# Loading the values of the first 14 attention heads over GpSimd's DMA queue instead of SyncE's

## The chip, the cores and the metric

The kernel runs on one core of a Trainium2 chip. Five engines work side by side: TensorE (PE, with its weight loads listed apart as PEld), VectorE (DVE), ScalarE (ACT), GpSimd (POOL) and SyncE (SP). SP does no arithmetic here; it issues transfers. The metric is device time in microseconds (us), the median of several runs.

## The reference, cut to what matters

Attention over 4 batches, 8 heads, 576 tokens and 64 numbers a head, with a causal mask and a decay bias, and behind it two feed-forward layers of 512 to 2048 to 512 over all 2304 tokens.

```python
scores = scale * q @ k.T
cum = cumsum(maximum(s, 0))
scores = where(causal, -1e9, scores + minimum(-(cum_i - cum_j), 0))
attn = softmax(scores)
x = (attn @ v) laid out as [B*S, H*D]
h = x @ w1_in;  x = (h * clip(h + 3, 0, 6) / 6) @ w1_out
h = x @ w2_in;  out = (h * sigmoid(h)) @ w2_out
```

## The kernel before, in words

Attention goes in head-parts: part A of a head is its first 256 query rows against the first 256 keys, part B the rest. The parts run in the order A0 A1 A2 B0 A3 B1 B2 B3 (the digit is the batch), eight heads each. A list of `Head` objects holds them, and a slot of the main loop carries one head through its stages while its neighbours are in other stages: the scores of the current head (`score`, L518), mask, scale and row maximum (`soft`, L540), exponentials (`expo`, L558), transposes of the head before (`trans`, L586), its product with the values (`av_whole`, L693), and the sum into the layer's input (L700, L711). In the same slot the heads two places ahead are loaded.

The first 9 slots carry heads only. From then on each slot also holds one step of the first feed-forward layer (`first`, L266 to L268, and `second`, L305 to L307), which takes most of TensorE's time. Weights arrive as 64-bit words, 512 KB a chunk (128 rows of 512), in `Chunk.load` (L147), and are turned into pairs of 32-bit parts by ScalarE (`fields`, L159, L160), GpSimd (L162) and VectorE (`join`, L178, L182, and `low`, L193). These ticks of the `Feed` are spread over the slots: three before the loop, 0.4 in each of the first nine slots, then two in each.

For the first 14 heads (`self.at < 14`) queries, keys and values go into one tile named `in...`, which lies in a place that weights will fill later; nothing has used it before, so the loads into it wait for no reader. A head's loads are the queries (L419), the keys (L420), the values (L409: 128 rows of 2 x 64 numbers, 64 KB) and, in `load_cum`, two rows that carry the decay (L429: from `pairs` in the on-chip memory for the first four heads, from `pair_d` in DRAM for the rest). The score matmul reads queries, keys and those two rows; only `av_whole`, a slot later, reads the values.

All loads so far go out on SP's queue, one after the other. The program is written through a layer that puts in the waits and that plans the order of each engine's instructions before the run, from the written order and from its own forecast of when each is ready. So what is ready early can stand early: the fills of `one` and `neg` in `split_rows` (L366, L367) are written behind the tenth slot. At run time every engine takes its instructions strictly in the planned order.

At the start 34 matmuls on a constant tile (`keep_clock`, L86) keep TensorE busy, and later slots without a feed-forward step add three each.

Of the kernel before, what the change touches and what calls it, by code (L numbers as in the profile page):

```python
# [27 lines left out]
def kernel(  # L28
# [15 lines left out]
    nc = tc.nc  # L44
# [85 lines left out]
    class Chunk:  # L130
# [10 lines left out]
        def load(self):  # L141
            if self.src.dtype == F32:
                self.val = self.place([P, DM], F32, "raw")
                nc.sync.dma_start(self.val, self.src)
            else:
                raw = self.place([P, 2 * DM], I32, "raw")
                nc.sync.dma_start(raw, self.src.bitcast(I32))  # L147
                words = raw.rearrange("p (n two) -> p n two", two=2)
                self.words = words[:, :, 0], words[:, :, 1]
# [226 lines left out]
    class Head:  # L376
# [23 lines left out]
        def load(self):  # L400
            b, h, nm, nk, nq = self.b, self.h, self.nm, self.nk, self.nq
            if self.at < 14:

                t = wpool.tile([P, 2 * DM], F32, tag=spare[self.at], name=f"in{nm}")
                self.q2, self.k2 = t[:, :nq], t[:, nq : nq + nk]
                self.qk = t[:, : nq + nk]
                self.va = t[:, DM + nk :][:, : self.nkc * D].rearrange("p (c d) -> p c d", d=D)
                self.load_qk()
                nc.sync.dma_start(self.va, v1[b, h, :, : self.nkc, :])  # L409
                return  # L410
            tags = ("qs", "kl") if self.whole and self.slot else ("q2", "k2")
            self.q2 = apool.tile([P, nq], F32, tag=tags[0], name=f"q2{nm}")
            self.k2 = apool.tile([P, nk], F32, tag=tags[1], name=f"k2{nm}")
            self.load_qk()
# [877 lines left out]
```

## Time and profile before

| what | us |
|---|---|
| median of 3 runs | 997.79 |
| lowest and highest run | 996.33, 1000.38 |
| time of the profiled execution | 999.31 |
| its span, first to last instruction | 997.5 |

| engine | busy us | share of the span |
|---|---|---|
| PE | 971.2 | 97% |
| PEld | 892.8 | 89% |
| DVE | 736.0 | 74% |
| ACT | 511.1 | 51% |
| POOL | 270.6 | 27% |

The first table holds the time to beat and what the profiled execution adds around its span (1.8 us). The second is an average over the whole run, over stages with different limits, so it does not tell what the first 45 us wait for; the changed loads all fall into those. SP has no busy time of its own; its issues stand in a timeline.

### The profile page before, as it was taken

The page shows a single profiled execution, that of the slowest core. Times are in us where ns is not written, and L with a number is a line of the kernel's source. Part 1 is how long each engine was busy: PE and PEld are TensorE (multiplying, and loading weights), DVE is VectorE, ACT ScalarE, POOL GpSimd, SP SyncE. Part 2 cuts the span into 40 slices and gives each one's busy share as a digit, 9 for nine tenths or more (in the row PEclk, how much of TensorE's full clock was granted, in tenths as well). Part 3 has the DMA queues.
Part 4 walks back from the last instruction along what each step waited for, and adds up shares of the span by engine and source line. Part 5 has one row for each costly group of instructions (what it writes and reads, how often), then busy time and mean ns, then how long its engine had stood idle before and what let it go on. Part 6 is the DMA issues. An engine that isn't in the chain of part 4 may idle for free.

```text
span 997.5 us, 17936 instructions
## 1 busy us (share of the span) xinstructions
PE 971.2 (97%) x6268; PEld 892.8 (89%) x6268; DVE 736.0 (74%) x1757; ACT 511.1 (51%) x1177; POOL 270.6 (27%) x323
## 2 busy tenths in 40 slices
PE   8899999999999999999999999999999999999997
PEld 5788899999999999999997877898988989889996
DVE  6899998898789888988867799887564434743343
ACT  5899655555455555545446656564443323432332
POOL 2123434343333434434325566532000000000000
PEclk8999999999999999999999999999999999999999
DMA  5785112212222222222215957434354233442421
GB/s 178 244 275 187 41 56 86 79 51 61 87 71 77 68 60 92 60 71 74 59 50 187 393 201 245 156 116 190 138 190 169 79 143 113 165 154 77 148 75 64
DMA packets 54419, 125.41 MB, mean 126 GB/s; under 512 B 12332, under 2 KB 34076, under 8 KB 51000
## 3 DMA queue, kind: packets, MB, share of 16 engines
q1 hardware_dynamic: 53880, 123.60, 36.8%
q8 instruction: 50, 0.82, 0.3%
q10 hardware_dynamic: 448, 0.66, 0.2%
q14 instruction: 41, 0.34, 0.1%
HBM read 99.52 MB, written 24.69 MB: 125 GB/s over the span
## 4 chain that ended last, share of the span: by engine, by line
PE 69%; DVE 11%; issue 7%; POOL 5%; DMA 4%; SPq 2%; ACT 1%; POOLq 0%; DVEq 0%; ACTq 0%
PE a L1089 6%; PE a L1090 6%; PE a L1091 6%; PE h L1072 5%; PE h L1074 5%; PE h L1073 5%; PE ph L266 4%; PE ph L267 4%; PE ph L268 4%; PE acc L306 4%; PE acc L305 4%; PE acc L307 4%; PE poB L678 3%; POOL rawo L167 2%; DMA rawi<-in_w2i_dram 2%
## 5 line engine op out<-in xcount | busy, mean ns | idle before, releaser
L266 PE MATMUL ph<-xh,wi 128*128 128x256 f32 (+1 forms) x512 | 152.7, 300 | 3.8 <-DVE g L279 3.6
L306 PE MATMUL acc<-gl,wo 128*128 128x256 f32 (+1 forms) x512 | 151.5, 298 | 1.4 <-DVE gl L286 1.4
L267 PE MATMUL ph<-xl,wi 128*128 128x256 f32 (+1 forms) x512 | 150.8, 295 | 0.3 <-DVE xl L732 0.3
L268 PE MATMUL ph<-xh,wi 128*128 128x256 f32 (+1 forms) x512 | 150.5, 294 | 0.0
L307 PE MATMUL acc<-gh,wo 128*128 128x256 f32 (+1 forms) x512 | 150.2, 295 | 0.0
L1131 ACT ACTIVATE gh<-h 128x384 fp32r<-128x384 f32 x96 | 50.3, 524 | 185.1 <-DVE h L1139 185.0
L305 PE MATMUL acc<-gh,wo 128*128 128x256 f32 (+1 forms) x512 | 143.4, 296 | 0.0
L1089 PE MATMUL a<-wo,gh 128*128 128x512 f32 x288 | 113.5, 394 | 1.4 <-ACT gh L1131 0.9
L1090 PE MATMUL a<-wo,gh 128*128 128x512 f32 x288 | 113.1, 393 | 0.0
L266 PEld LDWEIGHTS ph<-xh,wi 128*128 128x128 f32 x512 | 96.3, 188 | 9.1 <-DVE g L279 2.6
L306 PEld LDWEIGHTS acc<-gl,wo 128*128 128x128 f32 x512 | 96.5, 188 | 5.7 <-DVE gl L286 2.5
L267 PEld LDWEIGHTS ph<-xl,wi 128*128 128x128 f32 x512 | 96.4, 188 | 3.5 <-DVE xl L732 0.5
L307 PEld LDWEIGHTS acc<-gh,wo 128*128 128x128 f32 x512 | 96.5, 189 | 3.4
L268 PEld LDWEIGHTS ph<-xh,wi 128*128 128x128 f32 x512 | 96.5, 188 | 3.1
L305 PEld LDWEIGHTS acc<-gh,wo 128*128 128x128 f32 x512 | 95.3, 188 | 3.6 <-DVE gh L122 0.2
L1091 PE MATMUL a<-wo,gl 128*128 128x512 f32 x288 | 90.0, 392 | 0.0
L1133 DVE TENSOR_TENSOR gl<-h,gh 128x384 fp32r<-128x384 f32 x96 | 53.8, 560 | 39.9 <-ACT h L1132 38.2
L1139 DVE TENSOR_TENSOR h<-h,u 128x384 f32<-128x384 f32 x72 | 40.1, 556 | 53.5 <-PE h L1074 53.2
L114 POOL TENSOR_SCALAR gh<-g 128x512 fp32r<-128x512 f32 x68 | 50.5, 745 | 100.6 <-DVE g L279 87.5
L1072 PE MATMUL h<-x0t,w 128*128 128x384 f32 x192 | 64.9, 338 | 0.7 <-DVE u L1139 0.7
L1073 PE MATMUL h<-x1t,w 128*128 128x384 f32 x192 | 64.9, 338 | 0.0
L1074 PE MATMUL h<-x0t,w 128*128 128x384 f32 x192 | 64.7, 337 | 0.0
(222 smaller groups left out, 2522.6 us busy)
## 6 DMA issues: line engine op xcount, KB each, us to landing
w<-w_d SPq DMA_DIRECT2D x18, 1792.0 KB
w_d<-w SPq DMA_DIRECT2D x8, 1792.0 KB
k2B<-in_kT_dram SPq DMA_DIRECT2D x64, 144.0 KB
rawi<-in_w1i_dram SPq DMA_DIRECT2D x16, 512.0 KB
rawo<-in_w1o_dram SPq DMA_DIRECT2D x16, 512.0 KB
rawi<-in_w2i_dram SPq DMA_DIRECT2D x16, 512.0 KB
rawo<-in_w2o_dram SPq DMA_DIRECT2D x16, 512.0 KB
q2B<-in_qT_dram SPq DMA_DIRECT2D x64, 80.0 KB
```

The source lines that it names most:

```text
L266: nc.tensor.matmul(o, wih[:, cs], xh[c], start=c == 0, stop=False)
L267: nc.tensor.matmul(o, wih[:, cs], xl[c], start=False, stop=False)
L268: nc.tensor.matmul(o, wil[:, cs], xh[c], start=False, stop=c == NDC - 1)
L305: nc.tensor.matmul(a, woh[:, cs], gh[:, jj, :], start=b0, stop=False)
L306: nc.tensor.matmul(a, woh[:, cs], gl[:, jj, :], start=False, stop=False)
L307: nc.tensor.matmul(a, wol[:, cs], gh[:, jj, :], start=False, stop=b1)
L1072: nc.tensor.matmul(ps, w[:, 0, cs], xh[:, c, :], start=c == 0, stop=False)
L1073: nc.tensor.matmul(ps, w[:, 0, cs], xl[:, c, :], start=False, stop=False)
L1074: nc.tensor.matmul(ps, w[:, 1, cs], xh[:, c, :], start=False, stop=c == 1)
L1089: nc.tensor.matmul(accs[t], gh[:, k, cs], woh, start=b0, stop=False)
L1090: nc.tensor.matmul(accs[t], gh[:, k, cs], wol, start=False, stop=False)
L1091: nc.tensor.matmul(accs[t], gl[:, k, cs], woh, start=False, stop=b1)
```

## The change: which engine issues the load of the values

For the 14 heads, the load of the values is issued by GpSimd instead of SyncE. Source, destination and size stay the same, and so do all other loads.

```diff
                 self.load_qk()
-                nc.sync.dma_start(self.va, v1[b, h, :, : self.nkc, :])
+                nc.gpsimd.dma_start(self.va, v1[b, h, :, : self.nkc, :])
                 return
```

## Rows read from the trace of the kernel before

**Rows 1.** Busy time of each engine by stage: us busy (instructions), granted clock, DMA share, GB/s.
```profile
10.00:20.00 10.00, 7.86 (x47) 5.36 (x46) 9.04 (x34) 8.78 (x26) 1.90 (x3) 0.98 0.57 172
20.00:30.00 10.00, 9.62 (x52) 8.63 (x53) 6.37 (x26) 6.82 (x21) 1.25 (x2) 0.68 0.53 146
30.00:45.00 15.00, 12.32 (x92) 10.77 (x91) 12.38 (x50) 13.34 (x40) 2.49 (x4) 1.00 0.83 265
60.00:80.00 20.00, 18.48 (x144) 17.45 (x145) 19.84 (x61) 19.04 (x48) 4.29 (x6) 1.00 0.88 292
80.00:120.00 40.00, 37.16 (x305) 35.44 (x304) 38.70 (x93) 29.66 (x70) 14.95 (x19) 1.00 0.32 105
120.00:200.00 80.00, 78.94 (x652) 77.55 (x650) 71.68 (x198) 44.12 (x113) 30.84 (x46) 1.00 0.24 70
```

**Rows 2.** SP's issues in order of time: start, duration, line, tile loaded.
```profile
2.44 0.58 SPq L409 DMA_DIRECT2D inA<-in_v_dram  x1
4.22 0.58 SPq L409 DMA_DIRECT2D inA<-in_v_dram  x1
4.85 0.43 SPq L147 DMA_DIRECT2D rawi<-in_w1i_dram  x1
...
6.41 1.39 SPq L429 DMA_DIRECT2D inA<-pairs  x2
...
11.26 0.48 SPq L419 DMA_DIRECT2D inA<-in_qT_dram  x1
...
15.54 0.43 SPq L147 DMA_DIRECT2D rawo<-in_w1o_dram  x1
16.01 0.29 SPq L429 DMA_DIRECT2D inA<-pair_d  x1
...
19.62 0.58 SPq L409 DMA_DIRECT2D inA<-in_v_dram  x1
```

**Rows 3.** The changed line: durations minimum, median, maximum in ns, first and last start.
```profile
L409 SPq DMA_DIRECT2D inA<-in_v_dram x14: 578/584/1502, 2.4 to 43.3; - x14
```

**Rows 4.** The chain that ended last, two pieces of its first 60 us: start, duration.
```profile
5.80 5.44 DMA rawi<-in_w1i_dram
...
15.54 4.06 DMA rawo<-in_w1o_dram
```

**Rows 5.** All engines in order of time; in brackets the idle time before and its releaser.
```profile
2.89 0.50 POOL L96 TENSOR_SCALAR_AFFINE_SELECT cmask<-cmask 128x128 f32<-128x128 f32 x1
...
4.66 0.74 DVE L355 COPY pairs<-orow 32x256 f32<-32x256 f32 x1
4.68 0.57 POOL L367 MEMSET neg<- 32x576 f32 x1 [0.77 <-DVE orow L351]
...
9.77 0.67 POOL L162 TENSOR_SCALAR rawi<-rawi 128x512 f32<-128x512 f32 x1 [4.53 <-DMA rawo<-in_w1o_dram]
...
10.48 0.69 DVE L178 SCALAR_TENSOR_TENSOR magi<-magi,rawi 128x512 int32<-128x512 int32 x1 [4.07 <-POOL rawi L162]
...
11.24 0.30 PEld L518 LDWEIGHTS ps0A<-inA 66*128 66x128 f32 x2 [0.56 <-DMA rawi<-in_w1i_dram]
...
19.76 0.77 PE L518 MATMUL ps0A<-inA 66*128 66x128 f32 x2 [0.93 <-DVE wi L193]
```

**Rows 6.** Busy time of each engine in shorter stretches, columns as in the first group.
```profile
2.00:4.00 2.00, 2.00 (x7) 0.62 (x5) 1.30 (x2) 0.01 (x1) 1.91 (x5) 1.00 0.38 107
8.00:10.00 2.00, 2.00 (x11) 0.94 (x10) 0.00 (x0) 1.46 (x3) 0.23 (x1) 1.00 1.03 395
...
18.00:20.00 2.00, 0.74 (x4) 0.46 (x4) 1.55 (x9) 1.28 (x4) 0.00 (x0) 0.91 0.74 237
18.00:28.00 10.00, 8.74 (x43) 7.61 (x42) 6.46 (x30) 6.26 (x18) 0.65 (x1) 0.66 0.55 166
20.00:26.00 6.00, 6.00 (x25) 5.33 (x26) 3.44 (x14) 3.30 (x12) 0.65 (x1) 0.50 0.56 166
```

**Rows 7.** The second step of VectorE's join before 40 us: durations minimum, median, maximum in ns.
```profile
L182 DVE CUSTOM_DVE_ANT_0 magi<-rawi,magi x3: 680/684/1074, 11.2 to 31.7; 128x1024 uint16<-128x1024 uint16 x3
```

## The prediction, made before the change was run

> **What bounds the kernel now.** First I read the busy time by stage. From 120 us on TensorE has hardly any idle time (78.94 of 80 us), and from 60 to 120 us VectorE has hardly any (19.84 of 20, 38.70 of 40) [rows 1]. These two stages are long and the changed loads do not lie in them. The loads lie between 2.4 and 43.3 us [rows 3], and there no engine is full: VectorE works 9.04, 6.37 and 12.38 us in the stretches of 10, 10 and 15 us, so it stands idle for 7.2 us of the 35 [rows 1]. As VectorE is the limit right behind this stage and TensorE right behind that, a microsecond won or lost before 45 us should reach the end nearly whole, and nothing won elsewhere would.
>
> So the question is what the first 45 us wait for. The timeline of SP's queue is the second view: issue stands behind issue, about 0.04 us apart, and a load of values costs 0.584 us of it in the median [rows 3]. The chain of waits says the same: between the starts of two weight chunks it runs through SP's own issues, not through arithmetic, and it holds two transfers, one from 5.80 to 11.24 and one from 15.54 to 19.60 [rows 4]. Twice an SP issue starts as such a transfer ends, at 11.26 and at 19.62 [rows 2, 4]; each is the eighth issue behind that weight chunk, so I read it as a limit of eight transfers under way on this queue.
>
> The third view is the timeline of all engines around these two moments. The first scores start at 11.24, as the last of three weight chunks lands [rows 4, 5]; the decay rows they need were issued at 6.41, behind those chunks [rows 2]. The scores of the fifth head start at 19.76 after 0.93 us of an idle TensorE [rows 5]. The profile names a VectorE instruction as releaser, but the decay rows of this head were issued at 16.01, right behind the chunk that lands at 19.60 [rows 2, 4], and I hold that transfer for the cause. In that stretch TensorE had worked only 0.74 of 2 us, and from 20 to 26 us its granted clock is 0.50, the level of 1.2 GHz instead of 2.4, with TensorE busy 6.00 of 6 us and VectorE only 3.44 [rows 6].
>
> **The change, part by part.** Removed: 14 issues of 0.584 us and a gap of 0.04 us, 8.7 us of SP's queue in all [rows 3]. What of it lies on the path goes by where they stand.
>
> *The start.* Two loads of values stand ahead of the first weight chunk at 4.85 [rows 2]. Without them the chunks go out 2 x 0.62 = 1.2 us earlier, and the decay rows at 5.4 instead of 6.41, as VectorE's copy into their source ends at 4.66 + 0.74 = 5.40 [rows 2, 5]. At 2 to 4 us the transfers run at 107 GB/s with the DMA engines busy 0.38 of the time, at 8 to 10 us at 395 GB/s with a share of 1.03 [rows 6]: the start of the scores is set by when these chunks enter and by what shares the engines with them. That takes something back. A values load waits for nothing, and the planned order puts ready work early on POOL: its fill for a far later slot runs at 4.68 [rows 5]. So I expect POOL to issue several of the 14 loads before 10 us. At 64 KB each and 395 GB/s one costs 0.17 us of the full DMA engines; six more than now cost 1.0 us. The first scores come between 1.2 and 0.2 us earlier. I take 0.6.
>
> *The fifth head.* Five values loads stand ahead of the chunk at 15.54, so it and the decay rows behind it go out up to 5 x 0.62 = 3.1 us earlier. The decay rows then land at about 16.6 and TensorE need not stand idle at 18.8. That is 0.9 us. If TensorE then also stays at the upper clock, its 6.00 us of work at half clock shrink by up to 3.0. Both together are bounded by VectorE, whose idle time from 18 to 28 us is 10 - 6.46 = 3.5 us [rows 6]. So the term lies between 0.9 and 3.5; I take 2.4, nearer to the upper end, because TensorE's work in the stretch is full while VectorE's is not.
>
> *Behind 28 us.* VectorE stands idle for another 2.6 us from 30 to 45 [rows 1], but SP's queue has caught up there and the DMA share is 0.83, so faster issue finds fewer free engines. I take 0, and 2.6 for the far end of the range.
>
> Added: 14 issues on POOL. No row shows one. Below stands the same transfer on SP, 0.584 us in the median, above SP's slowest one, 1.50 us [rows 3]. I take 1.0, between them, thus 14 us on an engine that works 1.90, 1.25 and 2.49 us of the 35 from 10 to 45 [rows 1]. So the room is there, and I cost the added issues at nothing; what hides them is POOL's idle time, and the price where they stand ahead of POOL's part of the weights is the first slower rival below. The page DMA: Bandwidth & Descriptors of the Trainium skill, section Specifications, gives a first byte after about 1 us from GpSimd and 0.6 us from SP; by that, as an estimate, POOL's sum would be 14 us too, and no run here shows it yet.
>
> The values themselves are needed last: the product reads them a slot behind the scores, so even some microseconds of delay on POOL's queue lie behind the head's other stages.
>
> The sum is 0.6 + 2.4 = 3.0 us, made against this execution's 999.31 us (its span of 997.5 and 1.8 around it), so 996.3. The median of the runs is 997.79, 1.5 lower; on that scale the forecast is 994.8.
>
> **The rivals.**
>
> *Hidden anyway (997.2).* The clock falls nevertheless, because TensorE has too little to do before 20 us whatever the loads do, or the planned order changes and gives the time back; only the 0.6 at the start stays. For it speaks that VectorE is already busy 9.04 of 10 us just before [rows 1], so scores ready earlier wait for it too. Against it speaks the idle TensorE at 19.76.
>
> *All idle time filled (991.1).* 0.6 + 3.5 + 2.6 = 6.7 us. For it speaks that VectorE's list of work is fixed and that SP paced everything before 31 us; against it the DMA share of 0.83 to 0.88 behind 30 us.
>
> *POOL comes late (slower, about 1002).* VectorE's join at 10.48 waits for POOL's instruction at 9.77 [rows 5], and VectorE's order is fixed, so all masks and scores behind it stand too. POOL's fills with a bearing on this end at 2.89 + 0.50 = 3.39, so there are 6.4 us of room. With n values loads planned ahead of that instruction and t us for one, it decides from n x t = 6.4: with 7 ahead from t = 0.91, with all 14 from 0.46. With 7 at 1.50 the delay is 4.1 us (1001.9); with 14 at 1.0 it is 7.6 (1005.4). Against it: the order is planned with POOL's part of the weights as the older work, which goes first once it is ready.
>
> *VectorE is held by POOL (slower, 1003).* VectorE's copy at 4.66 takes 0.74 us and ends just after POOL's fill beside it (4.68 + 0.57 = 5.25) [rows 5], and a step of the join takes 1074 ns once beside 684 in the median [rows 7]. If each of the 14 loads costs VectorE the 0.39 us between these two, that is 5.5 us. The Trainium skill, page SBUF — State Buffer, section Who interferes with whom, has a rule that goes the same way: descriptor generation on GpSimd and those VectorE modes that use both ports exclude each other, so that whichever starts second waits. By it the load could also be the one that waits. The copy at 4.66 agrees with the rule; for a load no run here shows it yet. Against the rival: most of VectorE's long instructions here have two inputs or read TensorE's results, and the copy is the one full-width copy of its kind.
>
> **How the numbers follow.** Chances: forecast 0.45, hidden 0.26, all filled 0.12, POOL late 0.13, VectorE held 0.04. The bound for a difference that a measurement of this kernel can tell is 0.5%, 5 us (the three runs differ by 0.4%): 992.8 and 1002.8. The forecast's own bounds run from 1.1 us (0.2 + 0.9) to 4.7 us (1.2 + 3.5), 996.7 to 993.1; a fifth of it may fall under 992.8 with the noise of a median. With all filled that makes 0.21 faster. Of the slower rivals some end just under 1002.8: 0.13 slower, and 0.66 the same. The range reaches from 990.0 (a little beyond all filled) to 1001.5 (POOL late by a little less than 4.1 us).
>
> **What would show it.** Right: 14 issues on POOL, most before 25 us, of about 1 us each; the first weight chunk issued at 3.6 and the first scores at about 10.6; the fifth head's scores without an idle TensorE ahead of them; a granted clock near 1.00 from 20 to 26 us; VectorE idle under 2 us from 18 to 28, and the stage from 60 to 120 us the same length, only earlier. Wrong: a join of VectorE that waits for POOL for longer than now, a values load that TensorE's product waits for, a clock that falls elsewhere, or a later stage in another order with gaps of its own.

## The result and the profile after

The changed kernel takes 1008.53 us (median of 4 runs, 1004.49 to 1011.66) against 997.30 for the kernel before in the same comparison: a ratio of 1.0103, 95% interval 1.0074 to 1.0132. The forecast was 994.8 with a range up to 1001.5, so the change is slower by 1% where no measurable difference was forecast, and the time lies outside the range. The profiled execution of after took 1006.26 us, 6.95 more than that of before.

The changed line first: instances, durations in ns, first and last start, and the time from issue to landing. Its counterpart of before is [rows 3].

```profile
L409 POOL DMA_DIRECT2D inA<-in_v_dram x14: 534/534/745, 3.3 to 13.8; - x14
...
DMA to landing us min/median/max: 2.0/4.7/5.8
```

POOL in order of time (start, duration, idle time before it). [rows 5] has its weight instruction L162 at 9.77.

```profile
3.35 4.45 POOL L409 DMA_DIRECT2D inA<-in_v_dram  x8
8.18 0.53 POOL L409 DMA_DIRECT2D inA<-in_v_dram  x1 [0.38 <-issue]
10.13 0.53 POOL L409 DMA_DIRECT2D inA<-in_v_dram  x1 [1.43 <-issue]
11.21 1.08 POOL L409 DMA_DIRECT2D inA<-in_v_dram  x2 [0.54 <-issue]
...
13.32 1.06 POOL L409 DMA_DIRECT2D inA<-in_v_dram  x2
14.40 0.68 POOL L162 TENSOR_SCALAR rawi<-rawi 128x512 f32<-128x512 f32 x1
15.03 0.67 POOL L162 TENSOR_SCALAR rawo<-rawo 128x512 f32<-128x512 f32 x1
15.65 0.65 POOL L162 TENSOR_SCALAR rawi<-rawi 128x512 f32<-128x512 f32 x1
```

All 14 loads stand ahead of POOL's first weight instruction. Eight go out back to back; POOL stands idle before the ninth, tenth and eleventh, 2.3 us in all.

SP's issues, in the places of [rows 2]: the first weight chunk at 3.72 (4.85 before), the fourth at 14.12 (15.54).

```profile
3.72 0.59 SPq L147 DMA_DIRECT2D rawi<-in_w1i_dram  x1
...
5.44 1.40 SPq L429 DMA_DIRECT2D inA<-pairs  x2
...
14.12 0.59 SPq L147 DMA_DIRECT2D rawo<-in_w1o_dram  x1
```

SP is relieved as intended. Yet the first scores start at 11.22, where they started at 11.24 [rows 5]; and the chain of waits holds a transfer of 6.94 us from 4.82 where [rows 4] has 5.44 us from 5.80:

```profile
11.22 0.30 PEld L518 LDWEIGHTS ps0A<-inA 66*128 66x128 f32 x2 [1.22 <-DMA inA<-pairs]
```

```profile
4.82 6.94 DMA rawi<-in_w1i_dram
```

VectorE in order of time shows the largest difference:

```profile
11.86 0.29 DVE L540 CUSTOM_DVE_ANT_0 pb0A<-ps0A,cmask 128x128 f32<-128x128 f32 x1 [5.45 <-PE ps0A L518]
...
14.57 0.29 DVE L540 CUSTOM_DVE_ANT_0 pb0A<-ps0A,cmask 128x128 f32<-128x128 f32 x1 [1.30 <-PE ps0A L518]
...
17.68 0.42 DVE L540 CUSTOM_DVE_ANT_0 pb1A<-ps1A,cmask 128x256 f32<-128x256 f32 x1 [1.15 <-PE ps1A L518]
...
24.15 0.69 DVE L178 SCALAR_TENSOR_TENSOR magi<-magi,rawi 128x512 int32<-128x512 int32 x1
24.75 0.69 DVE L178 SCALAR_TENSOR_TENSOR mago<-mago,rawo 128x512 int32<-128x512 int32 x1
```

The first join of weights stood at 10.48 [rows 5] and now stands at 24.15, behind the scores of the first seven heads. It does not wait for POOL there: POOL was done with that chunk at 15.08, and no idle time stands before the join. Its place in VectorE's planned order has changed. In the meantime VectorE waits for scores, three times for more than a microsecond.

Busy time by stage, columns as in [rows 1] (PE, PEld, DVE, ACT, POOL, granted clock, DMA share, GB/s):

```profile
10.00:20.00 10.00, 7.99 (x44) 6.16 (x42) 4.25 (x24) 7.25 (x23) 5.58 (x10) 0.83 0.75 216
20.00:30.00 10.00, 9.18 (x64) 7.31 (x62) 9.19 (x37) 7.68 (x24) 0.00 (x0) 0.92 0.68 210
30.00:45.00 15.00, 12.31 (x63) 10.46 (x63) 14.53 (x45) 13.41 (x35) 4.60 (x6) 0.73 0.92 278
45.00:60.00 15.00, 12.10 (x56) 11.16 (x55) 15.00 (x41) 14.81 (x37) 3.25 (x4) 0.53 1.01 370
60.00:80.00 20.00, 16.82 (x133) 15.46 (x132) 19.97 (x53) 19.41 (x44) 5.64 (x8) 1.00 0.73 249
80.00:120.00 40.00, 36.19 (x295) 34.61 (x295) 39.88 (x105) 28.53 (x73) 12.54 (x15) 1.00 0.13 36
120.00:200.00 80.00, 79.88 (x667) 78.96 (x666) 67.54 (x181) 39.04 (x100) 30.99 (x42) 1.00 0.25 70
```

VectorE works 4.25 of the ten us from 10 to 20, where it worked 9.04. From there to 80 us it is nearly full (14.53 of 15 from 30 to 45, before 12.38). The granted clock from 30 to 45 and from 45 to 60 is 0.73 and 0.53; before it was 1.00 from 30 to 45 [rows 1] and beyond, as rows below show.

The whole stretch from 10 to 60 us, before and then after:

```profile
10.00:60.00 50.00, 43.13 (x287) 36.69 (x285) 42.76 (x149) 42.76 (x116) 9.29 (x13) 0.93 0.73 223
```

```profile
10.00:60.00 50.00, 41.59 (x222) 35.09 (x220) 42.97 (x144) 43.16 (x116) 13.44 (x20) 0.73 0.87 280
```

VectorE does as much work by 60 us as before, 42.97 us of it where it did 42.76. What differs is what that work is: the weight steps L178, L182 and L193 take 9.69, 8.02 and 8.54 us where they took 8.19, 8.25 and 7.54, and the heads get less. TensorE loses 1.5 us of busy time and runs at a mean granted clock of 0.73 instead of 0.93.

How the two are linked is to be seen at 34 to 38 us. VectorE:

```profile
33.98 1.16 DVE L178 SCALAR_TENSOR_TENSOR magi<-magi,rawi 128x512 int32<-128x512 int32 x1
35.07 0.68 DVE L182 CUSTOM_DVE_ANT_0 mago<-rawo,mago 128x1024 uint16<-128x1024 uint16 x1
35.67 0.28 DVE L700 TENSOR_TENSOR xtA<-poA,sums 128x128 f32<-128x128 f32 x1
35.87 0.68 DVE L178 SCALAR_TENSOR_TENSOR mago<-mago,rawo 128x512 int32<-128x512 int32 x1
...
36.54 0.68 DVE L182 CUSTOM_DVE_ANT_0 magi<-rawi,magi 128x1024 uint16<-128x1024 uint16 x1
37.14 0.41 DVE L122 COPY xA<-pxA 128x256 f32<-128x256 f32 x1
```

TensorE beside it:

```profile
36.00 0.44 PE L711 MATMUL pxA<-ident,xtA 128*128 128x128 f32 x2 [1.08 <-DVE xtA L700]
37.61 0.33 PE L586 MATMUL pt0A<-ident,pb0A 128*128 128x128 f32 x1 [0.84 <-DVE xA L122]
```

The head's small VectorE steps (L700, L122) stand behind late weight work (L178, L182), and TensorE waits for them. From 30 to 62 us it waits 5.4 us for these two where it waited 2.4 (for VectorE in all 5.4 and 3.9). It does not wait for the fuller transfers (DMA share 1.01 from 45 to 60): from 30 to 125 us TensorE waits for no transfer at all, before for 0.3 us. Shorter stretches, after and then before:

```profile
34.00:38.00 4.00, 2.08 (x14) 1.51 (x13) 4.00 (x9) 3.22 (x10) 0.60 (x1) 1.00 0.80 222
38.00:58.00 20.00, 16.39 (x68) 14.39 (x67) 19.69 (x56) 19.41 (x48) 4.86 (x6) 0.52 1.02 363
```

```profile
38.00:58.00 20.00, 16.32 (x122) 14.55 (x121) 18.93 (x55) 18.51 (x47) 4.95 (x6) 1.00 0.87 277
```

After TensorE had worked 2.08 of 4 us, the granted clock fell to 0.52 in the mean of the next 20 us, that is to 1.2 GHz for nearly all of them. TensorE is busy for the same time there, 16.39 and 16.32 us, and 68 matmuls stand in its record instead of 122. 16.39 x (1 - 0.52) = 7.9 us of full-speed work are missing after this stretch.

Following the same instructions through both traces: the scores of heads five to eight come 1 to 4 us earlier than before. The products with the values (L693) are on par at 31 us, and the one that ran at 41.8 runs at 48.9, 7.1 us late. The first feed-forward step is late by 9.2 (rows of its gate, the ScalarE instruction that reads its product, before and then after):

```profile
L278 ACT ACTIVATE g<-ph,half x13: 452/466/688, 44.0 to 119.5; 128x256 f32<-128x256 f32 x8, 128x512 f32<-128x512 f32 x5
```

```profile
L278 ACT ACTIVATE g<-ph,half x11: 452/472/691, 53.3 to 117.0; 128x256 f32<-128x256 f32 x8, 128x512 f32<-128x512 f32 x3
```

Up to 215 us the steps stay late by 8 to 13.5 us while the heads catch up; from 260 us on, where TensorE is full, the lag is 7.1 us, and the two spans differ by 6.9. TensorE's idle time and low clock, summed up in the next section, exceed those of before only up to 120 us, so this execution's loss is made there. The other 4 us between the medians lie in executions without a profile.

### The profile page after: what moved, and what is told of

The parts are those of the page before. It is cut to its first block, busy times and chain, and to the rows that moved or that the text cites. A ratio compares the mean times of both kernels' runs of the same rounds, so it can differ in the third digit from the quotient of the medians.

```text
span 1004.5 us, 18006 instructions
## 1 busy us (share of the span) xinstructions
PE 975.5 (97%) x6268; PEld 898.3 (89%) x6268; DVE 737.4 (73%) x1757; ACT 510.6 (51%) x1177; POOL 279.3 (28%) x337
## 4 chain that ended last, share of the span: by engine, by line
PE 73%; DVE 11%; DMA 6%; issue 4%; POOL 3%; SPq 2%; ACT 1%; DVEq 0%; POOLq 0%; ACTq 0%
PE a L1089 6%; PE a L1090 6%; PE a L1091 6%; PE h L1072 5%; PE h L1074 5%; PE h L1073 5%; PE ph L266 5%; PE ph L267 5%; PE acc L306 5%; PE ph L268 4%; PE acc L307 4%; PE acc L305 4%; PE poB L678 4%; POOL rawo L167 2%; DMA rawi<-in_w2i_dram 2%
## 5 line engine op out<-in xcount | busy, mean ns | idle before, releaser
L266 PEld LDWEIGHTS ph<-xh,wi 128*128 128x128 f32 x512 | 97.4, 190 | 7.0 <-DVE g L279 2.3
L268 PEld LDWEIGHTS ph<-xh,wi 128*128 128x128 f32 x512 | 97.6, 191 | 3.1
```

The costliest lines, as they stand in the source:

```text
L266: nc.tensor.matmul(o, wih[:, cs], xh[c], start=c == 0, stop=False)
L268: nc.tensor.matmul(o, wil[:, cs], xh[c], start=False, stop=c == NDC - 1)
```

## Experiments

Ratios are to the kernel before, with 95% intervals. For each profile I also sum what TensorE loses from 10 to 280 us: in stretches of 2 us, its idle time and its busy time x (1 - granted clock). Before this is 16.1 us (12.8 idle and 3.3 at the low clock, 1.2 GHz), after it is 27.2 (15.5 and 11.7). The sum is a rough measure: its difference is 11.1 us where these two executions differ by 6.95, and that the medians differ by 11.2 does not confirm it. By this measure most of the loss, 8.4 of 11.1, is made at the low clock.

**Only the order on POOL undone.** The loads stay on GpSimd but stand behind its weight instruction written last (`last_pool` holds it; the line that sets it is left out here).

```diff
+with tc.issue_after(last_pool[0].ins) if last_pool else ExitStack():
     nc.gpsimd.dma_start(self.va, v1[b, h, :, : self.nkc, :])
```

> All 14 values loads on GpSimd as in the change, but each load written after a GpSimd weight instruction (L162) is planned behind it, so VectorE's joins of the first weight chunks stand again ahead of or between the first heads' scores. Theory order (the planned order costs the time): VectorE busy over 8 us between 10 and 20 us, 994 to 999 us, no slower than before. Theory queue (a load issued by GpSimd itself costs the time, by its descriptors or its lateness): 14 such loads as in the change, so 1004 to 1010 us. Theory SP (SyncE running ahead costs the time): also 1004 to 1010 us.

Measured: 1005.42 us, 1.0073 [1.0052, 1.0095]. The first join is back at 9.6 us, so it was the loads standing ahead of POOL's weight work that had moved it:

```profile
9.61 0.69 DVE L179 SCALAR_TENSOR_TENSOR magi<-magi,rawi 128x512 int32<-128x512 int32 x1 [3.20 <-DMA inA<-pairs]
```

(The join is L179 in this run.) But the time did not come back: the theory of the order missed, and the time lies in the range of the two theories that blame the loads on GpSimd or SP's relief. VectorE is at work for 6.52 us from 10 to 20, not for the 8 that were expected. It has 11 halves of weights (L193, the last step of a chunk's preparation) ahead of the first step where before had 6 and the changed kernel 9, and TensorE is at the low clock for 20.5 us between 30 and 60.

**Only the loads on POOL added.** SP loads the values as before; GpSimd loads as many bytes into a place that nobody reads.

```diff
 nc.sync.dma_start(self.va, v1[b, h, :, : self.nkc, :])
+spare_v = t[:, DM : DM + self.nkc * D].rearrange("p (c d) -> p c d", d=D)
+nc.gpsimd.dma_start(spare_v, v1[b, h, :, : self.nkc, :])
```

> Values loaded by SyncE as before; in addition GpSimd issues 14 loads of the same size into an unused part of the same tiles. VectorE's first join is planned behind the scores of five heads. Theory order: slower than before though SyncE does all it did, 1001 to 1008 us, VectorE idle over 3 us between 10 and 20 us. Theory queue: slower too, 1003 to 1010 us. Theory SP: as before, 995 to 1000 us.

Measured: 1006.26 us, 1.0074 [1.0048, 1.0100]. The theory of SP's relief (995 to 1000) missed. The first join starts at 26.8 us, the first step is 9.4 us late (changed kernel 9.2), and the stages resemble those of the changed kernel:

```profile
10.00:20.00 10.00, 6.93 (x30) 5.26 (x29) 3.04 (x17) 6.69 (x20) 5.00 (x9) 0.75 0.71 203
...
30.00:45.00 15.00, 11.38 (x77) 8.77 (x76) 15.00 (x55) 13.63 (x41) 3.39 (x4) 1.00 0.77 222
45.00:60.00 15.00, 12.97 (x57) 11.27 (x55) 14.60 (x43) 14.98 (x38) 4.94 (x6) 0.54 1.01 326
```

So the loads on POOL are enough for most of the loss, without SP's relief. With one caution: this run moves 0.9 MB more than the others.

**Only SP relieved.** The 14 loads are left out; the product with the values reads the mask instead, so these heads' output is not attention.

```diff
-nc.sync.dma_start(self.va, v1[b, h, :, : self.nkc, :])
+self.va = cmask[:, : self.nkc * D].rearrange("p (c d) -> p c d", d=D)
```

> No load of values for the 14 heads at all; the product reads the mask tile in their place, so SyncE has 14 issues less and GpSimd none more. VectorE's joins are planned ahead of the scores as before. Theory order: 993 to 998 us, about the 3 us faster that were forecast. Theory queue: the same. Theory SP: slower, 1004 to 1010 us, as SyncE runs ahead just as in the change.

Measured: 1001.63 us, 1.0046 [1.0025, 1.0067]. Without any of the 8.7 us of issue that the change takes from SP the kernel is not faster; the time lies between the expected ranges, and all three theories missed. Here too 11 halves of weights stand ahead of the first step, which starts 4.9 us late; its lag from 260 us on is only 0.6, so the profile shows little of the 4 us, and where the rest is lost stays open.

**Only VectorE's order changed.** The loads are as before; VectorE's joins of the first four chunks are held behind the softmax reduction (L540) written last (`last_soft`; the line that sets it is left out). The condition goes by the chunk's number alone, so it also holds the first four chunks of the second layer, hundreds of us later.

```diff
+with tc.issue_after(last_soft[0].ins) if self.key[2] < 2 else ExitStack():
     nc.vector.scalar_tensor_tensor(out=mag, in0=mag, scalar=3, in1=high, ...)
```

> Values loaded by SyncE as before and nothing new on GpSimd; only VectorE's joins of the first four weight chunks are planned behind the scores written before them, so that the first join comes behind six heads as in the change (there seven). Theory order: slower, 1002 to 1010 us, with VectorE idle over 4 us between 10 and 20 us. Theories queue and SP: as before, 995 to 1000 us.

Measured: 1005.64 us, 1.0073 [1.0048, 1.0097], with no load on POOL at all. The first join starts at 22.7; VectorE works 4.68 us from 10 to 20 and is nearly full from 30:

```profile
10.00:20.00 10.00, 9.03 (x61) 6.72 (x60) 4.68 (x27) 7.19 (x23) 1.95 (x3) 1.00 0.59 174
...
30.00:45.00 15.00, 11.80 (x75) 9.57 (x74) 14.38 (x48) 13.67 (x38) 2.63 (x4) 0.87 0.84 257
45.00:60.00 15.00, 14.04 (x103) 13.56 (x102) 15.00 (x42) 13.63 (x32) 2.88 (x5) 0.90 0.99 306
```

So an order of VectorE's alone can cost 0.7%, here with only 6.8 us at the low clock between 30 and 60. But it does not cost it where the change does. The first step comes 2.9 us earlier than before, the next seven are on time or up to 2.0 us early, and the ninth is 5.0 us late. From 80 to 90 us TensorE works 5.88 us (before 9.36) and waits for a transfer of values (L695 is L693 of the other kernels):

```profile
80.00:90.00 10.00, 5.88 (x43) 5.36 (x43) 9.14 (x21) 6.75 (x16) 2.45 (x3) 0.94 0.43 139
```

```profile
87.92 0.85 PE L695 MATMUL poA<-vaA,thA 128*128 128x64 f32 x6 [3.37 <-DMA vaA<-in_v_dram]
```

The run shows how much an order can cost, not that the change's loss goes this way.

**TensorE's gaps filled.** In the changed kernel, 12 (later 36) short matmuls stand ahead of the product with the values of heads 8 to 15; the same fill goes into the kernel without the loads (which leaves out what it left out) and, as a control, into the kernel before.

```diff
+if 8 <= self.at < 16:
+    const = ident.bitcast(BF16)[:, :P]
+    for _ in range(12):
+        nc.tensor.matmul(po.rearrange("p c d -> p (c d)"), const, const, start=True, stop=True)
```

> The change, and in the products of heads 8 to 15 TensorE runs 12 short matmuls on a constant first, so that it has work between 35 and 60 us; VectorE's planned order stays nearly the same. Theory clock (the fall of the granted clock between 28 and 60 us costs the time): the clock stays near 1.00 there and the time falls to 998 to 1003 us. Theory order (VectorE has too much weight work planned ahead of the first steps, and the clock only follows the starved TensorE): 1005 to 1010 us, whatever the clock does.

> The kernel without the 14 loads of values (the product reads the mask tile), with the same 12 short matmuls in the products of heads 8 to 15. Theory clock: 995 to 999 us, below the 1001.6 us without the filling. Theory order: 1000 to 1004 us, as the first feed-forward step still stands behind ten weight halves instead of six.

> The kernel before with the same 12 short matmuls ahead of the product with the values of heads 8 to 15. Theory A (the fill gave back time that the changed kernels had lost, at the place where TensorE idled): before had no low clock between 30 and 60 us, so the fill can only add its own work, 996 to 1000 us, against 997.5. Theory B (the fill moves the rest of the plan, whatever stood ahead of it, so that its gain in the two other kernels says nothing of the start): 992 to 995 us, the 2 to 6 us that it gave there.

> The changed kernel with 36 instead of 12 short matmuls ahead of the product with the values of heads 8 to 15. The smaller fill left TensorE at the low clock from 39 to 55 us. Theory A (the low clock is a cause of its own: TensorE with its gaps filled stays at 2.4 GHz, and the steps that then run at the full clock give time back): fewer than 5 us at the low clock between 30 and 60, and 997 to 1001 us. Theory B (the low clock only follows from VectorE being late, and is paid while TensorE waits anyway): the clock stays up as well, but the first step's gate comes no earlier than in the changed kernel (53 us) and the time is 1003 to 1008 us, the smaller fill's gain gone into 18 us of filling.

Measured: after with 12, 1002.05 us, 1.0043 [1.0021, 1.0064]; without the loads and with the fill 999.41, 1.0024 [0.9998, 1.0049]; before with the fill 1004.22, 1.0071 [1.0045, 1.0096]; after with 36, 1018.00, 1.0195 [1.0137, 1.0254]. The fill gives the changed kernel 6 us and costs the kernel before 7, so it is no improvement of its own; both expectations for the control missed, as did both for 36, and the time without the loads lies between its two. With 12 the changed kernel's time lies in the range of the clock theory, but its condition, a clock near 1.00, did not come true: 17.0 us at the low clock between 30 and 60, where the changed kernel has 22.4. With 36 a window shows

```profile
39.00:50.00 11.00, 10.52 (x64) 9.56 (x64) 10.36 (x33) 10.34 (x26) 2.44 (x4) 0.51 1.02 322
```

The first step stayed about as late as in the changed kernel (8.7 us with 12, 9.2 with 36), and with 36 the filling came on top. Whether the low clock is a cause of its own or follows from the late heads is not settled by these runs.

**Weights held back.** The loads on GpSimd behind its weight work, as in the first experiment, with VectorE's joins from the second group of chunks on held behind the softmax; and the kernel before with the joins from the fourth group on held (`1 <= self.key[2]` and `3 <= self.key[2]` in the line of the fourth experiment, for the first layer).

> All 14 loads on GpSimd, planned behind its weight instructions as in pool_pinned, and VectorE's joins from the second weight chunk on planned no earlier than the scores written before them. Eight weight halves then stand ahead of the first step, and 12 ahead of the third to fifth, where pool_pinned has 11 and 15 to 18 and before 6 and 9 to 12. Theory order: 998 to 1003 us, below pool_pinned's 1005.4. Theory queue (a load issued by GpSimd costs the time itself): 1004 to 1008 us.

> The kernel before, the loads as they were, with VectorE's joins of the first layer's chunks from the fourth on held behind the last softmax reduction written so far, so that the weights stand a little later against the heads than before: 6, 8, 8, 10 halves ahead of the first four steps instead of 6, 8, 9, 11. Theory A (before stands near the best balance of heads and weights): 996 to 1000 us. Theory B (any later weight helps, as it did with the loads on GpSimd, by 3 us): 993 to 996 us.

Measured: 1002.06 us, 1.0037 [1.0014, 1.0060], in the range of the order theory, a gain of 3 us over the first experiment with intervals that just overlap; and 1001.63, 1.0040 [1.0020, 1.0059], a loss of 4 against before that neither theory expected. Moving weights back gained where 11 halves stood ahead of the first step and lost where 6 did: neither earlier nor later beat the order of before. With all 14 loads on POOL the first of the two is no slower than the kernel without any of them (1.0046), so no run shows a price of such loads apart from what they do to the order.

**Fewer loads, and another engine.** The first two or the first six loads alone on GpSimd (`self.at < 2`, `self.at < 6`, the others on SP); and all 14 on ScalarE (`nc.scalar.dma_start`).

> Only the values of heads 0 and 1 go over GpSimd. VectorE's planned order is nearly that of before, six weight halves ahead of the first step. The first weight chunk goes out 1.2 us earlier and no other values are pulled ahead. Theory order: 994 to 999 us, the first scores near 10.3 us. Theory queue: 997 to 1000 us, since two loads cost a seventh of the loss at most.

> GpSimd's queue takes the values of heads 0 to 5 alone; the other eight stay on SyncE's. Theory A (the cost is the order that is planned for the first 60 us): VectorE's first join stands behind the scores of one head or two more than before, but 11 halves of weights stand ahead of the first step instead of 6, as in the kernel without the loads: 1000 to 1004 us. Theory B (the cost goes by the number of loads issued by GpSimd, some 0.8 us each): 6 loads give 997.5 + 4.7 = 1002.2 us, and two gave 997.5 + 1.6 = 999.1. The two differ little in time; the lag of the first step against the heads tells them apart: under A the heads stay on par to the eighth and the step is late by 4 us or more, under B both are late alike.

> The values of the 14 heads issued by ScalarE instead of GpSimd. Theory A (SyncE's relief lets weights be planned ahead of heads, whichever engine takes the loads; GpSimd's own order is a second cost): VectorE's first join stands where it did before, 13 halves of weights stand ahead of the first step instead of 6, and the time is that of the kernel without the loads or somewhat more, 1000 to 1004 us. Theory B (the cost is GpSimd's alone: its queue or its weight instruction): 995 to 999 us. Theory C (ScalarE's own instructions come late behind 14 issues of 0.5 us, and it prepares weights too): 1005 to 1010 us, with the first join behind 15 us.

Measured: two 999.73 us, 1.0010 [0.9987, 1.0032]; six 1009.73, 1.0125 [1.0102, 1.0149]; ScalarE 1013.04, 1.0166 [1.0143, 1.0190]. Six loads cost as much as 14, so the cost does not go by their number, and it was also underestimated: both expectations for six missed, and all three for ScalarE; two lies in the range of the queue theory and 0.7 us above that of the order. With six the first join is at 12.3 us, 11 halves stand ahead of the first step, and the loss begins earlier:

```profile
20.00:30.00 10.00, 10.00 (x42) 8.17 (x41) 7.80 (x31) 7.34 (x23) 1.29 (x2) 0.50 0.67 186
...
45.00:60.00 15.00, 13.03 (x50) 10.62 (x50) 14.22 (x39) 14.49 (x37) 3.72 (x6) 0.50 1.03 365
```

Ten us at the low clock from 20 to 30 with TensorE full, where before had it from 20 to 26 [rows 6]; the seventh head's product with the values, at 36 us in before, is 7.4 us late. On ScalarE the issues hold up its own weight work, which the profile shows directly: five issues last 6.09 us, and the first `fields` runs at 11.55 (8.5 before).

```profile
5.42 6.09 ACTq L409 DMA_DIRECT2D inA<-in_v_dram  x5
11.55 0.67 ACT L159 ACTIVATE rawi<-rawi 128x512 int32<-128x512 uint32 x1 [5.74 <-DMA inA<-in_v_dram]
```

**VectorE relieved.** Both kernels without the second step of the join (L182) for the first layer; this leaves out the lowest three bits of those weights. It takes away 32 operations of 0.68 us, 21.8 us of VectorE (the expectation below counts too few).

```diff
-nc.vector.tensor_tensor(out=mag, in0=mag, in1=low, op=ALU.add)
+if self.key[1] != 0:
+    nc.vector.tensor_tensor(out=mag, in0=mag, in1=low, op=ALU.add)
```

> The changed kernel without the second step of VectorE's join (0.68 us each) for the 8 chunks of the first layer; it leaves out the lowest three bits of these weights. VectorE's order at the start stays as in the changed kernel (first join behind the scores of the seventh head). Theory A (the loss is VectorE's work, which piles up at 24 to 60 us because it was idle at 10 to 20): with 16 fewer such operations, 11 us of VectorE's work, most of it in that stretch, the time falls to 996 to 1002 us. Theory B (the loss is TensorE's alone, through its gaps at 10 to 40 and the clock): 1005 to 1010 us, as before the cut.

> The kernel before with the same cut, the control of the other. Theory A (VectorE is full from 45 us on here too, but not late): 994 to 998 us, so that the two lean kernels lie within 5 us of each other. Theory B (VectorE's work sets nothing in the first 60 us): 997 us, and the two lie 8 us or more apart, as without the cut.

Measured: changed kernel 1002.46 us, 1.0040 [1.0017, 1.0063]; kernel before 1000.71, 1.0022 [0.9998, 1.0047]. Relieved of this work the two lie 1.7 us apart instead of 11, with overlapping intervals, and their lags from 260 us on are the same 2.2 us. The first join of the changed one still stands late, at 22.8 us. The cut gives the changed kernel 6 us, with all 14 loads still on POOL, so much of its loss hangs on VectorE's weight work. That all of it does is not shown, for the control is not clean. The cut shifts the plan too: from 30 to 125 us TensorE waits 6.1 us for transfers in the kernel before with the cut, 0.3 without it, and 2.5 in the changed kernel with the cut. The kernel before lost 2 us by the cut, and some of the closeness of the two comes from there. Both times lie above the first theory's ranges, though within the 5 us of each other that it expected. Both kernels spend 20.5 us at the low clock between 10 and 200 us.

**The profiles of the kernels without fill** (us; lag is that of the steps behind 260 us; lost is TensorE's sum as above; both belong to one execution, the ratio to the medians):

| kernel | ratio | lost | low clock, 30 to 60 | lag |
|---|---|---|---|---|
| before | 1 | 16.1 | 0 | 0 |
| first two | 1.0010 | 21.6 | 3.4 | 2.2 |
| before, lean | 1.0022 | 22.1 | 10.2 | 2.2 |
| behind POOL's weights, held | 1.0037 | 25.6 | 23.0 | 5.6 |
| held from fourth | 1.0040 | 19.6 | 10.2 | 2.4 |
| after, lean | 1.0040 | 22.5 | 13.6 | 2.2 |
| no loads | 1.0046 | 18.8 | 17.0 | 0.6 |
| behind POOL's weights | 1.0073 | 25.9 | 20.5 | 5.8 |
| late joins | 1.0073 | 20.9 | 6.8 | 4.9 |
| extra loads | 1.0074 | 27.2 | 13.6 | 8.4 |
| after | 1.0103 | 27.2 | 22.4 | 7.1 |
| first six | 1.0125 | 28.6 | 19.8 | 10.5 |
| ScalarE | 1.0166 | 35.3 | 19.8 | 13.6 |

The lag grows with the lost time, late joins apart. In this table only the kernel before spends no time at 1.2 GHz between 30 and 60 us. No kernel tried has a median below that of the kernel before.

## Why the prediction was wrong

The step that failed is "I cost the added issues at nothing", and with it the assumption that VectorE's list of work is fixed. POOL's idle time hides its issues in the sense of busy time. But the order is planned before the run: 14 loads that are ready at once stand ahead of POOL's weight instruction, the joins that need it stand behind seven heads on VectorE, and a VectorE that was busy 9.04 of 10 us becomes idle for 5.75 of them. Its weight work then falls into the 40 us behind, between the heads' steps and into the stretch that the prediction itself had named as VectorE's limit. TensorE waits 5.4 us for those steps from 30 to 62 us, where it waited 2.4, and has the low clock for 22.4 us between 30 and 60.

Point by point:

- **The start, -0.6: measured 0.** SP did issue the first chunk at 3.72 (3.6 forecast). Part of the term went the way of "something back": eight values loads are out by 7.8 us instead of the two before, and a chunk's transfer in the chain takes 6.94 instead of 5.44 us. But it cannot be all, for the kernel without any of the 14 loads does not start earlier either (11.40). The term left out TensorE itself: its 34 `keep_clock` matmuls stand ahead of the scores and last until 11.18 in the kernel before and until 11.77 without the loads (rows in this order). Their end lies between 10.4 and 11.9 us in the runs here, and no run starts its scores before 11.1.

```profile
1.45 9.73 PE L86 MATMUL idle<-busy 128*128 128x512 bf16 x34 [1.45 <-DVE half L101]
```

```profile
1.44 10.33 PE L86 MATMUL idle<-busy 128*128 128x512 bf16 x34 [1.44 <-DVE half L101]
```

- **The fifth head and the clock, -2.4: not gained.** The dip at 20 to 26 us is gone and the scores of heads five to eight come earlier, but dips at 14.8 to 18.2 us (0.83 in the stage from 10 to 20) and at 28.5 to 31.9 came, and a long one from 38.7 to 59.2. The text named "a clock that falls elsewhere" as a sign of error; this was it.
- **Behind 28 us, 0: the whole loss lies there.** On par at 31 us, the heads' products are late by 7 to 11 us at 49 to 61.
- **A loss before 45 us reaches the end nearly whole:** only in part. Late by 9.2 us at the first gate and by up to 13.5 behind it, the steps are 7.1 us late from 260 us on.
- **SP as the pace of the start:** its timeline was read rightly, the conclusion was not. With SP's issues taken away altogether, the kernel is 0.46% slower.
- **POOL's price of 1.0 us an issue:** 0.534. The nearest row, SP's median of 0.584, would have served. The 1 us of the Trainium skill, page DMA: Bandwidth & Descriptors, section Specifications, is a latency to the first byte; POOL was held for half of that.
- **The rival "POOL comes late":** its condition came true, 14 x 0.534 = 7.5 us against 6.4, and POOL's weight instruction came 4.6 us later. Its mechanism did not: VectorE never waited for POOL. The lateness was planned, not met at run time. Its two times, 1001.9 and 1005.4, lie below the measured median. "The older work goes first once it is ready", held against it, was wrong.
- **The rival "Hidden anyway":** it alone named a changed plan, but only as one that gives the time back.
- **The rival "VectorE is held":** refuted. The copy beside the loads took 0.28 us (below), and the join at 9.61 in the first experiment took 0.69 us beside POOL's loads at 9.53 to 10.65, as in before [rows 5]; its second step at 12.20 took 0.69 us beside loads at 11.40 to 13.06, where 0.684 is the median [rows 7].

What is shown: the loads ahead of POOL's weight work move VectorE's first join from 10.48 to 24.15; loads on POOL added to those of SP cost 0.7% with as late a first step; SP's relief alone gains nothing; and 21.8 us less of weight work on VectorE gives the changed kernel 6 us. What is only argued: that the changed order makes the whole loss (with the order on POOL undone 0.7% remained, and the late joins lost their time elsewhere), and how much of it the low clock makes by itself. What stays open: why six loads cost as much as 14, beyond that the low clock came at 20 to 30 us and 11 halves stood ahead of the first step.

## What to carry to other kernels

Where a layer plans the order, a change of queue is also a change of plan: ask which instruction the moved work will stand ahead of on its new engine, who consumes that one's result, and where that consumer's work goes if the planner believes it late. An idle engine hides issue time but not a reordering. And a start in which two engines keep each other just busy is fragile: here each shift that was tried without fill, early or late, brought stretches at 1.2 GHz between 30 and 60 us. A control can lose in a new place what the change does not touch, so look for its own waits before comparing two times.

## What the runs showed of the hardware that was not expected

GpSimd's load of 64 KB holds POOL for 0.534 us. Eight went out back to back; the ninth to eleventh were each preceded by idle time (0.38, 1.43 and 0.54 us). A fixed limit of eight under way, as the prediction read for SP, is not shown by that: in the run with extra loads ten went out back to back before the first idle time, 1.04 us. The landings took 2.0, 4.7 and 5.8 us (least, median, most). The Trainium skill, page DMA: Bandwidth & Descriptors, section Anatomy of one DMA — SWDGE (gpsimd) path, fits a transfer's time by 2.0 us plus the bytes over 436 GB/s; for 64 KB that is 2.15 us as an estimate. The fastest landing, 2.0 us, agrees; the median is over twice that, in a stretch where the DMA engines were shared with weights and other loads (share 0.93 from 4 to 10 us, 0.75 from 10 to 20).

VectorE's copy at 4.66 us, which took 0.74 us beside a POOL fill [rows 5], stands amid POOL's eight issues in the changed kernel and is shorter:

```profile
4.66 0.28 DVE L355 COPY pairs<-orow 32x256 f32<-32x256 f32 x1
```

So the copy took 0.46 us longer beside the fill, and the loads did not hold it. Nor did it hold a load: the one issued beside it, at 4.62, took 0.534 us like the others. That copy and fill exclude each other fits the rule on ports that the prediction quoted (the Trainium skill, page SBUF — State Buffer, section Who interferes with whom); which of the two came first cannot be told from starts 0.02 us apart. That the generation of descriptors and VectorE block each other is not seen here. The slow step of [rows 7], 1074 ns at 11.21, ran beside POOL's weight instruction L162 at 11.09, not beside a load.
